# Quarter-array score products for left-over queries, and an earlier time table for the first batch, in a top-k attention and hard-swish kernel

## Chip, cores and metric

The kernel runs on one core of a Trainium2 chip. The metric is device time in microseconds (us); lower is better.

## The reference

Attention over 8 batches of 8 heads with 576 positions and a head dimension of 64, in float32, keeps only the 32 largest scores of each query; a two-layer feed-forward with a hard-swish follows.

```python
scores = scale * np.matmul(q, k.transpose(0, 1, 3, 2))
kth = np.partition(scores, -top_k, axis=-1)[..., -top_k:-top_k + 1]   # top_k = 32
scores = np.where(scores >= kth, scores, -1000000000.0)
attn = np.exp(scores - np.max(scores, axis=-1, keepdims=True))
attn = attn / (np.sum(attn, axis=-1, keepdims=True) + 1e-09)
x = np.matmul(attn, v)        # (B,H,S,D) -> (B*S, H*D) = (4608, 512)
h = x @ w_in                  # 512 -> 2048
g = h * np.clip(h + 3.0, 0.0, 6.0) / 6.0
out = g @ w_out               # 2048 -> 512
```

## The kernel before

**Pairs and duos.** A `Pair` is two heads of one batch: head 0 lies on partitions 0 to 63, head 1 on 64 to 127. Of 576 positions 512 make four tiles of 128 (J = 4), and R = 64 are left over. A `Duo` is two pairs (u = 0 and 1) and one tile of 128 queries, so it has four rows of 576 scores per partition; a left-over duo (`rest`, qt = J) holds the 64 left-over queries of both pairs' heads, head 0 on partitions 0 to 63 and head 1 on 64 to 127, so it has only two rows. A batch has 8 full and 2 left-over duos, 80 in all, numbered m. In batches 0 to 2 the two left-over duos are the batch's last (m = 8 and 9 in the first), in batches 3 to 6 they are spread, in the last they come early.

**The stages of a duo**, by engine: the scores on TensorE (PE) (`scores`; L215 and L217 for left-over duos, L226 and L232 for full ones) and their copy out of PSUM on ScalarE (ACT) (L219 and L220, L233 and L236); the top 32 on VectorE (DVE) in four rounds of MAX8 and MATCH_REPLACE8 (L250, L254); a shift on GpSimd (POOL) (L263, L266); Prelu and Exp with the sum on ACT (L273, L278, L283); the reciprocal on DVE (L287); the weights' product and a split into 16-bit halves on POOL (L297, L306); a DMA transpose on SP's queue (L312); joining the halves on ACT for u = 0 and on POOL for u = 1 (L318); the product with the values on PE (L338) and its copy on ACT (L348).

**The feed-forward** of a block of 128 tokens is 16 pieces: four times 32 products L365, ACT's L373 and L375 and POOL's gate L379 and L380, then 32 products of 128x512 (L385), the scaling on ACT (L395) and the store on SP (L397).

**The weights** arrive in a wide form and are converted in 32 chunks of 128x512 in the first 153 us, one step of each per slot: ACT takes the absolute value (L108) and a second part (L111), POOL clamps (L109), DVE shifts and merges (L117, L118), POOL adds (L123). The chunks' `a` and `y` tiles and the feed-forward's `g` share a pool of 8 buffers.

**Order.** Every engine works its instructions in the order in which the program issues them (`manual_schedule`). The main loop goes over the duos; each has 8 slots, in each of which DVE gets one round of top-k for one u (slots 0 to 3 for u = 0, 4 to 7 for u = 1). A full duo's slot takes some 2.4 us on DVE, a left-over duo's some 1.4 us. What follows a duo's top-k is written into tables by slot, counted from the duo's first: a stage at 9 is issued in slot 1 of the next duo. `early` holds for duos 0 and 1, `usual` for the rest of the first batch, `behind` (as `usual`, with the values at 25) for the middle, `soon` for the last two. In the first four duos all stages but the reciprocals and weights are issued before the slot's conversion step, these two after it. Feed-forward pieces are issued at a rate that follows how many are queued (`due`); what is left at the end follows without top-k beside it.

Of the kernel before, what the change touches and what calls it, by code (L numbers as in the profile page):

```python
# [29 lines left out]
def kernel(  # L30
# [9 lines left out]
    nc = tc.nc  # L40
    P = nc.NUM_PARTITIONS
    B, H, S, D = q.shape
    DM, FF = moe_w_in.shape
    J = S // P
    JP = J * P
    R = S - JP
# [41 lines left out]
    def big():  # L88

        return ps_big.tile([P, 5 * 512], F32, tag="big", name="big")  # L90
# [48 lines left out]
    class Pair:  # L139


        def __init__(self, b, hp):
            self.b, self.hp = b, hp
            self.vm, self.vr, self.kr = vms[hp], vrs[hp], krs[b % 2 * NHP + hp]
# [40 lines left out]
    class Duo:  # L185
# [3 lines left out]

        def __init__(self, pairs, qt):
            self.pairs, self.qt, self.early = pairs, qt, False
            self.rest = qt == J
            self.nt = 1 if self.rest else 2
            self.nb = J + 2 if self.rest else 2 * J + 1
            self.m, self.less = [None] * 2, [None] * 2
            self.e16, self.t16, self.eT = [None] * 2, [None] * 2, [None] * 2

        def scores(self, us=(0, 1)):  # L200

            if us[0] == 0:
                self.sc = scpool.tile([P, 2, 2 * (S + R)], F32, tag="sc", name="sc")
                self.den = mpool.tile([P, 2, 2], F32, tag="den", name="den")
            sc, nu = self.sc[:, us[0] : us[-1] + 1, :], len(us)
            ps = big()
            heads = [slice(0, D), slice(D, P)]
            qs = slice(self.qt * P, min(self.qt * P + P, S))
            banks = ps[:, 0 : 4 * 512].rearrange("p (n s) -> p n s", s=512)
            left = ps[:, 4 * 512 :]  # L210
            if self.rest:
                for i, u in enumerate(us):
                    pr = self.pairs[u]
                    for d in heads:
                        nc.tensor.matmul(banks[d, i, :], pr.qT[d, qs], pr.kT[d, :])  # L215
                    for hh, d in enumerate(heads):
                        nc.tensor.matmul(left[d, i * R : (i + 1) * R], pr.qT[d, qs], pr.kr[d, hh, :])  # L217
                nc.gpsimd.memset(sc[:, :, S : S + R], 0.0)
                nc.scalar.copy(sc[:, :, 0:JP], banks[:, 0:nu, :])  # L219
                nc.scalar.copy(  # L220
                    sc[:, :, JP:S], left[:, 0 : nu * R].rearrange("p (u r) -> p u r", r=R)
                )
                return
            for i, u in enumerate(us):
                pr = self.pairs[u]
                nc.tensor.matmul(  # L226
                    left[:, i * P : (i + 1) * P], pr.qT[:, qs], pr.kr[:].rearrange("p h r -> p (h r)")
                )
            for i, u in enumerate(us):
                pr = self.pairs[u]  # L230
                for hh, d in enumerate(heads):
                    nc.tensor.matmul(banks[:, 2 * i + hh, :], pr.qT[d, qs], pr.kT[d, :])  # L232
            nc.scalar.copy(  # L233
                sc.rearrange("p u (h s) -> p (u h) s", h=2)[:, :, 0:JP], banks[:, 0 : 2 * nu, :]
            )
            nc.scalar.copy(  # L236
                sc[:, :, JP : JP + P], left[:, 0 : nu * P].rearrange("p (u r) -> p u r", r=P)
            )
# [87 lines left out]
        def values(self, dst):  # L326

            w = R if self.rest else P
            pv = ps_w.tile([P, 512], F32, tag="w", name="pv")
            for u in range(2):  # L330
                pr, eT = self.pairs[u], self.eT[u]
                for c in range(J + 1):
                    for hh in range(2):
                        if self.rest:
                            rhs = eT[:, c if c < J else J + hh, hh * R : (hh + 1) * R]
                        else:
                            rhs = eT[:, c if hh == 0 or c == J else J + 1 + c, :]
                        nc.tensor.matmul(  # L338
                            pv[hh * D : (hh + 1) * D, u * w : (u + 1) * w],
                            pr.vm[:, hh, c, :] if c < J else pr.vr[:, hh, :],  # L340
                            rhs,
                            start=(c == 0),
                            stop=(c == J),
                        )
            self.pv = dst, pv[:, 0 : 2 * w].rearrange("p (u q) -> p u q", u=2)
# [70 lines left out]
    per_batch = 2 * J + 2  # L416
    ND = len(duos)
# [4 lines left out]
    left = 0  # L422
# [87 lines left out]
    def pair_at(m, first):  # L510

        b, at = divmod(m, per_batch)
        return pairs[b + 1][at - first] if b + 1 < B and 0 <= at - first < NHP else None
# [18 lines left out]
    usual = dict(  # L532
        shift0=3, exp0=4, inverse0=9, weights0=10, flip0=12, join0=15,
        shift1=7, exp1=8, inverse1=13, weights1=14, flip1=16, join1=19, values=22, place=23,
    )

    behind = dict(usual, values=25, place=26)
    early = dict(
        shift0=3, exp0=3, inverse0=4, weights0=4, flip0=5, join0=8,
        shift1=7, exp1=7, inverse1=8, weights1=8, flip1=9, join1=12, values=12, place=13,  # L540
    )
    soon = dict(
        shift0=3, exp0=3, inverse0=5, weights0=5, flip0=7, join0=10,
        shift1=7, exp1=7, inverse1=9, weights1=9, flip1=11, join1=14, values=16, place=17,
    )
    queued = {}
    for m in range(ND):
        for part, at in (early if m < 2 else soon if m >= ND - 2 else behind if per_batch <= m < ND - 4 else usual).items():
            queued.setdefault(8 * m + at, []).append((m, part))

    def parts(slot, late=None):

        for m, part in sorted(queued.get(slot, []), key=lambda x: x[1][:-1] != "shift"):
            if late is not None and (part[:-1] in ("inverse", "weights")) != late:
                continue
            if part == "values":
                values(m)
            elif part == "place":
                place(m)
            else:  # L560
                getattr(duos[m], part[:-1])(int(part[-1]))

    due = 0.0
    for m in range(ND + 3):
        u = duos[m] if m < ND else None
        for i in range(8):
# [18 lines left out]
            if i == 0:  # L585
                p = pair_at(m, 4)
# [5 lines left out]
            if i == 5:  # L592
                p = pair_at(m, 5)
# [42 lines left out]
```

## Time and profile before

| | us |
|---|---|
| median of 8 runs | 1581.54 (1580.07 to 1583.55) |
| the profiled execution | 1581.16 |
| its span in the profile | 1579.3 |
| DVE busy | 1467.0 (93%) |
| PE busy | 1455.3 (92%) |
| POOL busy | 1143.7 (72%) |
| ACT busy | 1096.0 (69%) |
| largest group: L250 MAX8 `m<-wk`, x864 | 613.6 |
| L385 MATMUL `acc<-w_out,g`, x1152 | 517.7 |
| L365 MATMUL `h<-xT,w_in`, x4096 | 483.1 |
| L215 MATMUL `big<-kq` 64x512, x128 | 32.8 |

How to read it: a float32 product leaves two MATMUL records, and their ends are modelled, so the time of one is better read from start to start. Engines work in order; a line of a timeline gives start, length, engine, source line, operation, tiles, shapes and count, and in brackets the idle time before it and the engine whose work ended that wait. Idle time of an engine counts only where what it delays is waited for in turn.

### The profile page before, as it was taken

The numbers are of one execution on the slowest core, as the hardware profiler recorded it, in microseconds if no ns is written. First come the engines' busy times: TensorE is split into PE (matmuls) and PEld (weight loads), VectorE is DVE, ScalarE is ACT, GpSimd is POOL, SyncE is SP. The second block draws the span as 40 slices with busy tenths as digits, with TensorE's granted clock in tenths as the row PEclk, the third lists the DMA queues.
The fourth block names the chain that finished last, engine by engine and source line by source line (L and its number), as shares of the span: only waits on it lengthen the run. The fifth ranks groups of instructions, "written<-read, shape, count | busy, mean of one in ns | idle before, by whom it ended". The sixth has DMA issues, their size and how long they took to land.

```text
span 1579.3 us, 28787 instructions
## 1 busy us (share of the span) xinstructions
PE 1455.3 (92%) x10272; PEld 1037.2 (66%) x10272; DVE 1467.0 (93%) x3105; ACT 1096.0 (69%) x1865; POOL 1143.7 (72%) x1264
## 2 busy tenths in 40 slices
PE   5355799879999999998999999999999999999899
PEld 3152666567767777776777777776777767677675
DVE  6999999999999999999999999999999999999700
ACT  6675777777776777777776786777766787777621
POOL 4868687777867777767687777777687777767841
PEclk9577899989999999999999999999999999999999
DMA  8652544444444543545244443446344443533400
GB/s 236 160 180 45 113 83 86 89 91 97 76 96 86 98 83 78 103 86 119 55 103 79 99 89 75 93 96 119 51 94 88 98 88 73 104 66 68 83 22 14
DMA packets 450319, 144.49 MB, mean 91 GB/s; under 512 B 433280, under 2 KB 441472, under 8 KB 450176
## 3 DMA queue, kind: packets, MB, share of 16 engines
q1 hardware_dynamic: 450176, 142.65, 43.2%
q8 instruction: 81, 1.33, 0.3%
q14 instruction: 62, 0.51, 0.1%
HBM read 45.09 MB, written 9.44 MB: 35 GB/s over the span
## 4 chain that ended last, share of the span: by engine, by line
DVE 50%; PE 38%; POOL 4%; issue 3%; ACT 2%; SPq 1%; DMA 1%; POOLq 0%; DVEq 0%; ACTq 0%
DVE m L250 26%; DVE wk L254 22%; PE h L365 15%; PE acc L385 14%; PE pv L338 4%; PE big L232 3%; DVE y L118 1%; POOL e L306 1%; PE big L177 1%; DVE a L117 1%; POOL sc L297 1%; POOL eT L318 1%; PE big L215 1%; ACT sc L278 1%; PE big L226 1%
## 5 line engine op out<-in xcount | busy, mean ns | idle before, releaser
L250 DVE MAX8 m<-wk 128x8 f32<-128x576 f32 x864 | 613.6, 747 | 2.2
L385 PE MATMUL acc<-w_out,g 128*128 128x512 f32 x1152 | 517.7, 601 | 17.1 <-POOL g L380 17.1
L365 PE MATMUL h<-xT,w_in 128*128 128x128 f32 x4096 | 483.1, 279 | 17.3 <-ACT xT L348 17.3
L365 PEld LDWEIGHTS h<-xT,w_in 128*128 128x128 f32 x4096 | 472.7, 194 | 39.6 <-issue 18.7
L254 DVE MATCH_REPLACE8 wk<-m,wk 128x576 f32<-128x576 f32 x576 | 424.0, 743 | 0.0
L385 PEld LDWEIGHTS acc<-w_out,g 128*128 128x128 f32 x1152 | 213.7, 191 | 263.8 <-issue 239.4
L297 POOL TENSOR_SCALAR sc<-sc,den 128x576 f32<-128x576 f32 x288 | 213.5, 752 | 219.7 <-DVE den L287 212.6
L306 POOL COPY e<-sc 128x2304 uint16<-128x2304 uint16 (+1 forms) x192 | 320.2, 1678 | 10.1
L278 ACT ACTIVATE sc<-sc,shift 128x576 f32<-128x576 f32 x288 | 220.4, 769 | 35.8 <-POOL shift L266 32.8
L318 ACT COPY eT<-t 128x2304 uint16<-128x2304 uint16 (+1 forms) x82 | 215.9, 2633 | 36.5 <-DMA t<-e 35.6
L273 ACT ACTIVATE sc<-sc,m 128x576 f32<-128x576 f32 x288 | 210.1, 777 | 44.5 <-DVE m L250 44.4
L338 PE MATMUL pv<-eT,vm 128*64 128x128 f32 (+1 forms) x2560 | 163.3, 272 | 55.3 <-ACT eT L318 43.9
L254 DVE MATCH_REPLACE8 wk<-m,sc 128x576 f32<-128x576 f32 x288 | 212.0, 743 | 0.0
L318 POOL COPY eT<-t 128x2304 uint16<-128x2304 uint16 (+1 forms) x78 | 203.8, 2612 | 6.9 <-DMA t<-e 6.6
L250 DVE MAX8 m<-sc 128x8 f32<-128x576 f32 x288 | 203.4, 743 | 1.9 <-ACT sc L236 1.9
L338 PEld LDWEIGHTS pv<-eT,vm 128*64 128x64 f32 x2560 | 134.4, 140 | 106.7 <-ACT eT L318 49.7
L373 ACT ACTIVATE g<-h,three 128x512 f32<-128x512 f32 x144 | 98.5, 684 | 150.4 <-PE h L365 139.7
L380 POOL TENSOR_TENSOR g<-g,hs 128x512 f32<-128x512 f32 x144 | 184.9, 1284 | 12.1 <-POOL g L379 0.2
L379 POOL TENSOR_SCALAR g<-g 128x512 f32<-128x512 f32 x144 | 89.2, 619 | 75.0 <-ACT g L373 65.4
L233 ACT COPY sc<-big 128x2048 f32<-128x2048 f32 (+1 forms) x65 | 119.3, 1836 | 27.3 <-PE big L232 27.2
L232 PE MATMUL big<-kq 64*128 64x512 f32 x512 | 136.1, 652 | 0.0
L395 ACT ACTIVATE o<-acc 128x512 f32<-128x512 f32 x36 | 21.4, 595 | 109.9 <-PE acc L385 109.9
(47 smaller groups left out, 1115.9 us busy)
## 6 DMA issues: line engine op xcount, KB each, us to landing
landed<-in_k_dram SPq DMA_DIRECT2D x64, 128.0 KB, 2.8
landed<-in_q_dram SPq DMA_DIRECT2D x64, 128.0 KB, 2.9
st<-in_moe_w_in_dram SPq DMA_DIRECT2D x16, 512.0 KB, 5.0
vm<-in_v_dram SPq DMA_DIRECT2D x64, 128.0 KB, 2.3
st<-in_moe_w_out_dram SPq DMA_DIRECT2D x16, 512.0 KB, 6.6
out_dram<-o SPq DMA_DIRECT2D x32, 256.0 KB, 2.4
t<-e SPq DMA_TRANSPOSE x160, 4.6
landed<-in_k_dram SPq DMA_DIRECT2D x32, 32.0 KB, 2.6
```

Source lines behind the costliest of these rows:

```text
L232: nc.tensor.matmul(banks[:, 2 * i + hh, :], pr.qT[d, qs], pr.kT[d, :])
L250: nc.vector.max(self.m[u][:, t, 8 * r : 8 * r + 8], self.cur[t])
L254: nc.vector.match_replace(wk, self.m[u][:, t, 8 * r : 8 * r + 8], self.cur[t], LOWEST)
L273: nc.scalar.activation(row, row, AF.Prelu, bias=m[:, t, TOP_K - 1 : TOP_K], scale=-1.0, alpha=FLAT)
L278: nc.scalar.activation(row, row, AF.Exp, bias=self.less[u][:, t : t + 1], scale=-scale / FLAT, accum_out=self.den[:, u, t : t + 1],)
L297: nc.gpsimd.tensor_scalar(row, row, self.den[:, u, t : t + 1], 1.0, ALU.mult, ALU.mult)
L306: nc.gpsimd.tensor_copy(halves[:, :, to : to + c1 - c0], words)
L318: copy(eT[:, 0 : self.nb, :] .rearrange("p c q -> p (c q)") .bitcast(U16) .rearrange("p (x h) -> p h x", h=2), self.t16[u][:, 0 : 2 * self ...
L338: nc.tensor.matmul(pv[hh * D : (hh + 1) * D, u * w : (u + 1) * w], pr.vm[:, hh, c, :] if c < J else pr.vr[:, hh, :], rhs, start=(c == 0), ...
L365: nc.tensor.matmul(h[:, (f - f0) * P : (f - f0 + 1) * P], w_in[:, i, f * P : (f + 1) * P], xT[:, i, :], start=(i == 0), stop=(i == NHP - 1),)
L380: nc.gpsimd.tensor_tensor(g[:], g[:], hs[:], ALU.mult)
L385: nc.tensor.matmul(acc[:], gs[f // nf][:, f % nf * P : (f % nf + 1) * P], w_out[:, f, :], start=(f == 0), stop=(f == NFC - 1),)
```

## The change

Two edits.

**Scores of left-over duos.** Before, pair u wrote its two heads' products to bank u: rows 0 to 63 of the array to columns 0 to 63, and rows 64 to 127 to columns 64 to 127, pair after pair, each followed by its two small products into a fifth bank. Now the second pair's heads change places on the output (`heads[u ^ hh]`): its head 0 goes to columns 64 to 127 and its head 1 to columns 0 to 63. The four 64x512 products use the four quarters of the array and are issued one after another, then the four small ones, into banks 2 and 3. The rows of the second pair are therefore swapped, and `values` reads them back with `(u ^ hh)`.

**The table of the first batch.** Duos 2 to 9 get a table `tight` in place of `usual`. Duos 0 and 1 keep `early`; `behind`, `usual` and `soon` hold for the others as before.

```diff
             if self.rest:
-                for i, u in enumerate(us):
-                    pr = self.pairs[u]
-                    for d in heads:
-                        nc.tensor.matmul(banks[d, i, :], pr.qT[d, qs], pr.kT[d, :])
-                    for hh, d in enumerate(heads):
-                        nc.tensor.matmul(left[d, i * R : (i + 1) * R], pr.qT[d, qs], pr.kr[d, hh, :])
+                quarters = [
+                    (i, hh, d, heads[u ^ hh])
+                    for i, u in enumerate(us)
+                    for hh, d in enumerate(heads)
+                ]
+                for i, hh, d, to in quarters:
+                    pr = self.pairs[us[i]]
+                    nc.tensor.matmul(banks[to, i, :], pr.qT[d, qs], pr.kT[d, :])
+                for i, hh, d, to in quarters:
+                    pr = self.pairs[us[i]]
+                    nc.tensor.matmul(banks[to, 2 + i, 0:R], pr.qT[d, qs], pr.kr[d, hh, :])
                 nc.gpsimd.memset(sc[:, :, S : S + R], 0.0)
                 nc.scalar.copy(sc[:, :, 0:JP], banks[:, 0:nu, :])
-                nc.scalar.copy(
-                    sc[:, :, JP:S], left[:, 0 : nu * R].rearrange("p (u r) -> p u r", r=R)
-                )
+                nc.scalar.copy(sc[:, :, JP:S], banks[:, 2 : 2 + nu, 0:R])
...
-                            rhs = eT[:, c if c < J else J + hh, hh * R : (hh + 1) * R]
+                            rhs = eT[:, c if c < J else J + hh, (u ^ hh) * R :][:, 0:R]
...
+    tight = dict(
+        shift0=3, exp0=3, inverse0=8, weights0=8, flip0=10, join0=13,
+        shift1=7, exp1=7, inverse1=11, weights1=11, flip1=13, join1=16, values=19, place=20,
+    )
     queued = {}
     for m in range(ND):
-        for part, at in (early if m < 2 else soon if m >= ND - 2 else behind if per_batch <= m < ND - 4 else usual).items():
+        if m < per_batch:
+            when = early if m < 2 else tight
+        elif m < ND - 4:
+            when = behind
+        else:
+            when = soon if m >= ND - 2 else usual
+        for part, at in when.items():
             queued.setdefault(8 * m + at, []).append((m, part))
```

For comparison, the table that duos 2 to 9 had:

```python
usual = dict(
    shift0=3, exp0=4, inverse0=9, weights0=10, flip0=12, join0=15,
    shift1=7, exp1=8, inverse1=13, weights1=14, flip1=16, join1=19, values=22, place=23,
)
```

## The prediction

> **What bounds the kernel now.** I read the busy table by 40 us windows first, then VectorE's (DVE's) waits, then the timelines around each wait, then the end. Columns of the windows: stretch, length, busy us and count of PE, weight loads, DVE, ACT, POOL, then granted TensorE clock, DMA share, GB/s.
>
> ```profile
> 120.00:160.00 40.00, 22.45 (x64) 9.41 (x62) 36.69 (x74) 22.91 (x39) 32.56 (x33) 0.79 0.26 51
> ...
> 480.00:520.00 40.00, 40.00 (x277) 27.95 (x277) 40.00 (x87) 28.75 (x48) 29.40 (x32) 1.00 0.44 82
> ...
> 1520.00:1560.00 40.00, 40.00 (x270) 32.35 (x269) 0.00 (x0) 8.88 (x16) 12.16 (x14) 1.00 0.04 14
> ```
>
> In the middle PE and DVE are both full; at the end only PE works. Which of the two is the bound is told by DVE's idle times. These are all of them over 0.3 us between its first and its last top-k; the bracket holds the idle time before the instruction and who ended it.
>
> ```profile
> 137.07 1.48 DVE L117 TENSOR_SCALAR a<-a 128x512 uint32<-128x512 uint32 x1 [3.31 <-POOL a L109]
> ...
> 1181.26 0.17 DVE L287 RECIPROCAL den<-den 128x2 f32<-128x2 f32 x1 [1.02 <-ACT den L283]
> ...
> 1270.65 0.17 DVE L287 RECIPROCAL den<-den 128x2 f32<-128x2 f32 x1 [0.53 <-ACT den L283]
> ...
> 1372.19 0.16 DVE L287 RECIPROCAL den<-den 128x1 f32<-128x1 f32 x1 [1.46 <-ACT den L283]
> 1375.36 1.42 DVE L250 MAX8 m<-sc 128x8 f32<-128x576 f32 x2 [0.69 <-ACT sc L236]
> ```
>
> So from 13.5 us to the last top-k's end at 1492 us DVE is the bound: it loses 3.31 us once in the weight conversion and 3.70 us (1.02+0.53+1.46+0.69) late. The end hangs on it by a string of fixed length. In PE's timeline:
>
> ```profile
> 1496.56 1.25 PE L338 MATMUL pv<-eT,vm 128*64 128x128 f32 x16 [4.41 <-POOL eT L318]
> ```
>
> That POOL copy stands right behind the weights of the last duo on POOL's queue, and those wait for DVE's reciprocal at 1487.9. From 1496.6 on PE works some 80 us without a gap. The time is therefore DVE's arrival at its last duo plus a constant, as long as PE has its older work done (4.41 us in hand). What PE saves is worth only what it takes out of DVE's waits.
>
> **Part 1, four quarter products.** A left-over duo's scores on PE, before:
>
> ```profile
> 204.37 1.07 PE L215 MATMUL big<-kq 64*64 64x512 f32 x4
> 205.28 0.28 PE L217 MATMUL big<-kr,kq 64*64 64x64 f32 x4
> 205.40 1.03 PE L215 MATMUL big<-kq 64*64 64x512 f32 x4
> 206.26 0.28 PE L217 MATMUL big<-kr,kq 64*64 64x64 f32 x4
> 206.47 7.13 PE L385 MATMUL acc<-w_out,g 128*128 128x512 f32 x16
> ```
>
> A float32 product makes two records, so x4 is two products. Two of 64x512 take 0.91 us (204.37 to 205.28) and the next thing starts at 206.47: 2.10 us in all. One full-array 128x512 product takes 0.86 us (L385: 8 records in 3.44 us in the chain), so the two quarters (first rows to first columns, second to second) already run together. That two column halves run together on different moving data is shown by L338: 40 records, 20 products, in 2.33 us, 0.12 us each, where a 128-column L365 product takes 0.22 us (64 in 14.29 us). Four at once is shown nowhere. Bounds: all four overlap, about 0.95 us for the large and 0.12 for the small ones, 1.07 us, 1.03 us saved; or the second pair doesn't overlap the first, 2.10 us, nothing saved. Worse than nothing is excluded: the new order begins with the same two diagonal quarters side by side. Both halves of the evidence being in the trace, I take 1.03 us, x16 duos = 16.5 us of PE.
>
> The Trainium skill, "TensorEngine Tiling (Array Packing)", section "Gotcha 1: PSUM Pressure", says that different row tiles can't access the same PSUM bank at the same time. The old pair does put both row tiles into one bank (on different partitions) and takes 0.91 us, not 1.7, so the row speaks against the rule. By the rule the two products of a bank would not overlap, and the new order, whose neighbours share a bank, would save nothing: the sum would be that of the third rival.
>
> Of the 16.5 us the time sees only DVE's 3.70. PE has not idled between 1094 us and 1485; left-over scores stand at 1158, 1247, 1337 and 1355, so PE is 1, 2 and about 4 us early at the waits. At 1181 the reciprocal waits for exps behind ACT's output scaling, which waited 4.94 us for PE: 1.0 earlier covers 1.02. At 1270 the chain is PE h, ACT g, eT copy, exps: 2 us covers 0.53. At 1372 the value loads on SP's queue (1358.3 to 1362.8, released by PE's pv) hold up the transpose that feeds ACT's eT copy: 2 to 3 us earlier covers 1.46 and then 0.69. I take 3.4 of 3.7; bounds 0 and 3.7. The copies behind the scores keep their sizes (1.01 and 0.28 us) and are hidden on ACT.
>
> **Part 2, the tighter table, duos 2 to 9.** By the order listing it moves work only in the first 310 us: beyond the 675th matmul of 5282, the 241st POOL and the 367th DVE instruction the orders are the same but for the quarters; on SP one store and one transpose change places. PE's feed-forward starts earlier, but PE idles anyway until 327 us (9.31 us there), so that is worth nothing, and the tail holds the same work as before. What counts is DVE up to 310 us. Its one wait comes like this, on POOL and ACT:
>
> ```profile
> 125.66 2.15 POOL L297 TENSOR_SCALAR sc<-sc,den 128x576 f32<-128x576 f32 x2
> 127.87 2.10 POOL L306 COPY e<-sc 128x2304 uint16<-128x2304 uint16 x1
> 130.06 1.40 POOL L379 TENSOR_SCALAR g<-g 128x512 f32<-128x512 f32 x1
> 131.54 1.26 POOL L380 TENSOR_TENSOR g<-g,hs 128x512 f32<-128x512 f32 x1
> ...
> 134.54 0.69 ACT L373 ACTIVATE g<-h,three 128x512 f32<-128x512 f32 x1 [9.12 <-POOL w_out L123]
> ```
>
> POOL's weights and gate delay its add (L123, 133.2 to 134.5), which frees a buffer for ACT's g; behind g stands ACT's abs of a weight chunk (135.59), then POOL's clamp (136.42), then DVE's shift (137.07). After the change the same queue, walked with these durations: clamp to 116.1, weights (now two slots earlier) to 117.6, split to 119.7, gate to 121.7, add to 123.0; abs 0.7, clamp 0.6, add 1.3 to 125.6; ACT's score copies hold the next abs to 126.9; clamp, gate, shift, add to 131.3; ACT's g and hs to 132.6, 2.9 us earlier than before. But the exps of duo 3 now stand ahead of the abs (1.44, 1.9 and 0.2 us): 136.1, abs 136.7, clamp 137.3. DVE's wait stays, about 0.3 longer. Then the second half's weights of duo 2, three slots earlier, come between that clamp and the next add: 2.15 + 2.10 to 141.6, add 142.9, clamp 143.5; the next conversion on DVE, at 141.91 before, starts at 143.5. Cost 1.6 us. Bounds: -3.3 (the wait goes) and +4.3 (a whole weights and split, 2.15 + 2.10, added to it).
>
> The reciprocals move too: the second half's from five slots behind its exps to four, 9.7 us behind the top-k, or 5.6 where those slots are a left-over duo's. DVE then waits for ACT if den is later, and all later top-k queue behind it. Before, den came 2.6 to 5.8 us after the top-k's end in duos 4 to 7 (5.4 for duo 7: top-k ends at 221.8, den at 227.2) and 6.7 for the second half of duo 8. Against 9.7 that is covered; against 5.6, twice, it costs 0 to 1.1 each. I take 0.5, bounds 0 and 2.2.
>
> **Sum**, on the profiled execution (span 1579.3, 1581.16 with 1.9 outside it): 1579.3 - 3.4 + 1.6 + 0.5 = 1578.0, so 1579.9. The median of the 8 runs lies 0.4 above that execution: 1580.2.
>
> **Rivals.** Within 0.2% means 1578.4 to 1584.7, about what a measurement of this kernel can tell from no change.
> 1. Forecast, late waits go, the early queue gives some back: 1580.2; 0.32.
> 2. The early queue is no worse or loses its wait: -3.4 with 0 early gives 1578.1, -3.7 and -3.3 give 1574.5. For it: g is free 2.9 us earlier, and if the exps' 3.5 us ran beside something else the wait would be gone. Against: ACT is in order. 0.30.
> 3. The quarters run two at a time, the late waits stay: 1581.5 + 2.1 = 1583.6; 0.12, still within 0.2%.
> 4. Slower: the earlier reciprocals make DVE wait for ACT in the first batch. For it: the second half of duo 3 had its den 10.5 us after its top-k (144.18 to 154.66), more than the 9.7 now allowed. Price: 0.8 there, 2.2 at the left-over duos, up to 4.3 in the conversion: 7.3, less 3.4, is 1585.4; without the late gain 1588.8. It decides once the early loss passes 3.2 us plus what the late waits give. 0.26.
>
> So faster 0.30, same 0.44, slower 0.26. The range 1573.8 to 1586.0 leaves out the far part of case 4 and the edge of 2; case 1's own is 1578.4 to 1582.5.
>
> **What would show it.** Right: L215 at x8 in about 1.0 us; DVE's waits at 1181 to 1375 gone; DVE's wait for POOL's clamp still about 3.5 us; duo 4's first top-k (144.18) at 145 to 147; PE's last gap before pv at 4 us or more. Wrong: L215 x8 still near 2 us; new waits of DVE for den before 300 us over 1 us; a tail after that gap other than 80 us.

## The result, and the profile after

The changed kernel takes 1585.7 us (median of 11 runs, 1584.0 to 1586.5), the kernel before 1580.7 us (31 runs on the same chip): ratio 1.0030, 95% interval 1.0022 to 1.0037. It is slower by 0.3%. The profiled execution has a span of 1584.0 us (1579.3 before) and a granted TensorE clock of 0.956 (0.963 before).

**The quarters work.** In PE's timeline of the changed kernel a left-over duo's scores now look like this:

```profile
211.71 1.09 PE L222 MATMUL big<-kq 64*64 64x512 f32 x8
212.62 0.29 PE L225 MATMUL big<-kr,kq 64*64 64x64 f32 x8
212.84 3.70 PE L391 MATMUL acc<-w_out,g 128*128 128x512 f32 x8
```

Eight records, four products, from 211.71 to 212.62: 0.91 us, what two took before. The whole block takes 1.13 us to the next instruction, against 2.10 us.

**DVE lost time early and won it late.** All idle times of DVE over 0.3 us between 100 us and the last top-k, in DVE's timeline of the changed kernel (the bracket holds the idle time before the instruction):

```profile
125.28 1.48 DVE L117 TENSOR_SCALAR a<-a 128x512 uint32<-128x512 uint32 x1 [2.46 <-POOL a L109]
...
138.27 0.43 DVE L117 TENSOR_SCALAR a<-a 128x512 uint32<-128x512 uint32 x1 [4.17 <-POOL a L109]
...
144.68 0.43 DVE L117 TENSOR_SCALAR a<-a 128x512 uint32<-128x512 uint32 x1 [2.61 <-POOL a L109]
...
245.99 0.16 DVE L293 RECIPROCAL den<-den 128x1 f32<-128x1 f32 x1 [4.02 <-ACT den L289]
```

The four late waits at 1181 to 1375 us are gone (-3.70). In the conversion there are three waits, 9.24 us, in place of one of 3.31 (+5.93), and a new one of 4.02 us at the second half of duo 8. Sum: +6.25. The two conversion instructions themselves got shorter, 52.2 us busy in all against 55.2 (L117 and L118 in the groups by line), so about 3 us came back. Most of that had come back before the first wait, so the two nearly cancel: DVE is ready for the 29th of the 32 L117 at 122.82 us and, after 2.46 us, begins it at 125.28; before, it began it at 125.78 without a wait. The time is lost at the second and third waits: duo 4's first top-k begins at 147.37 us, before at 144.18. DVE ends its last top-k at 1495.7 us, before at 1492.2: +3.6. The rest of the span follows in 88.3 us (before 87.2).

Two stretches by windows show the place; the columns are those of the prediction's first fence:

```profile
120.00:160.00 40.00, 23.43 (x95) 11.73 (x94) 30.77 (x62) 21.27 (x33) 31.70 (x32) 0.80 0.23 45
...
1520.00:1560.00 40.00, 40.00 (x250) 30.26 (x247) 0.00 (x0) 8.03 (x15) 9.40 (x10) 1.00 0.04 14
```

Between 120 and 160 us DVE works 30.77 us instead of 36.69; the tail is full of PE work, as before.

**How the conversion waits come about.** POOL's timeline ahead of the first of them, changed kernel:

```profile
115.99 2.04 POOL L303 TENSOR_SCALAR sc<-sc,den 128x576 f32<-128x576 f32 x2
118.09 2.10 POOL L312 COPY e<-sc 128x2304 uint16<-128x2304 uint16 x1
120.28 0.67 POOL L385 TENSOR_SCALAR g<-g 128x512 f32<-128x512 f32 x1
121.03 1.59 POOL L386 TENSOR_TENSOR g<-g,hs 128x512 f32<-128x512 f32 x1
122.58 1.26 POOL L123 TENSOR_TENSOR w_out<-a,y 128x512 int32<-128x512 int32 x1
124.63 0.62 POOL L109 TENSOR_SCALAR a<-a 128x512 f32<-128x512 f32 x1 [0.79 <-ACT a L108]
```

Weights, split and gate stand ahead of the add (L123), which frees the buffer that ACT's abs needs; then come abs, clamp, and only then DVE. The second wait has another maker. ACT's timeline ahead of it:

```profile
132.66 0.69 ACT L379 ACTIVATE g<-h,three 128x512 f32<-128x512 f32 x1 [4.41 <-POOL w_out L123]
...
133.72 1.45 ACT L279 ACTIVATE sc<-sc,m 128x576 f32<-128x576 f32 x2
...
136.82 0.65 ACT L108 ACTIVATE a<-st 128x512 f32<-128x512 f32 x1
```

Between 133.72 and 136.82 ACT does the exps of duo 3, which the tight table puts one slot earlier, ahead of the abs: 3.1 us. The third is again POOL's: weights at 138.33, split at 140.61, add at 142.68, clamp at 144.03.

**How the wait at duo 8 comes about.** ACT's timeline, changed kernel:

```profile
239.86 2.79 ACT L324 COPY eT<-t 128x2304 uint16<-128x2304 uint16 x1 [1.27 <-DMA t<-e]
242.51 1.01 ACT L179 COPY kq<-big 128x1024 f32<-128x1024 f32 x1
...
243.98 0.78 ACT L279 ACTIVATE sc<-sc,m 128x576 f32<-128x576 f32 x1
...
245.75 0.20 ACT L289 ACTIVATE den<-den 128x1 f32<-128x1 f32 x1
```

The top-k of that half ended at 236.3 us. Its exps start at 243.98, because ACT's queue holds the join of duo 7 ahead of them, which waits for its DMA transpose, and behind the join the copies L179 to L183 (1.5 us). The same join stood ahead of the same exps before, as ACT's timeline of the kernel before shows, but there the exps followed it at once:

```profile
235.04 2.80 ACT L318 COPY eT<-t 128x2304 uint16<-128x2304 uint16 x1 [0.54 <-DMA t<-e]
237.71 0.77 ACT L273 ACTIVATE sc<-sc,m 128x576 f32<-128x576 f32 x1
```

There that top-k ended at 233.0 us. The join starts 3.6 us after the top-k in place of 2.0, and from its start to the exps it is 4.1 us in place of 2.7: together the 3.0 us by which den is later (9.7 us after the top-k, 6.7 before). The transpose is late because duo 7's weights began on POOL only at 231.59, 5.1 us after their reciprocal (226.50): a gate and another join stood ahead of them. POOL's timeline, changed kernel:

```profile
226.93 0.62 POOL L385 TENSOR_SCALAR g<-g 128x512 f32<-128x512 f32 x1 [1.27 <-ACT g L379]
...
228.84 2.80 POOL L324 COPY eT<-t 128x2304 uint16<-128x2304 uint16 x1
231.59 1.50 POOL L303 TENSOR_SCALAR sc<-sc,den 128x576 f32<-128x576 f32 x2
```

### The profile page after: what moved, and what is told of

It reads as the page before. It is cut to its first block, busy times and chain, and to the rows that moved or that the text cites. A ratio compares the mean times of both kernels' runs of the same rounds, so it can differ in the third digit from the quotient of the medians.

```text
span 1584.0 us, 28784 instructions
## 1 busy us (share of the span) xinstructions
PE 1445.6 (91%) x10272; PEld 1035.9 (65%) x10272; DVE 1464.2 (92%) x3105; ACT 1098.1 (69%) x1865; POOL 1144.9 (72%) x1264
## 4 chain that ended last, share of the span: by engine, by line
DVE 77%; PE 8%; POOL 6%; issue 4%; ACT 2%; SPq 1%; DMA 1%; POOLq 0%; ACTq 0%
DVE m L256 41%; DVE wk L260 36%; PE h L371 4%; PE acc L391 4%; POOL e L312 1%; POOL a L109 1%; POOL sc L303 1%; ACT sc L284 1%; PE pv L344 1%; POOL eT L324 1%; POOL w_in L123 1%; DVE den L293 1%; DMA st<-in_moe_w_in_dram 1%; POOL w_out L123 1%; SPq L151 0%
## 5 line engine op out<-in xcount | busy, mean ns | idle before, releaser
L371 PE MATMUL h<-xT,w_in 128*128 128x128 f32 x4096 | 487.5, 280 | 20.3 <-ACT xT L354 20.3
L371 PEld LDWEIGHTS h<-xT,w_in 128*128 128x128 f32 x4096 | 477.0, 196 | 42.0 <-ACT xT L354 21.6
L381 ACT COPY hs<-h 128x512 f32<-128x512 f32 x144 | 83.5, 580 | 0.0
```

The costliest lines, as they stand in the source:

```text
L371: nc.tensor.matmul(h[:, (f - f0) * P : (f - f0 + 1) * P], w_in[:, i, f * P : (f + 1) * P], xT[:, i, :], start=(i == 0), stop=(i == NHP - 1),)
```

## Experiments

Theory after the result: the two edits are independent; the quarters take DVE's late waits away, the table gives back more than that in the conversion and at duo 8. For each run: DVE's waits between 100 us and the last top-k, that top-k's end, and what follows it to the end of the span, all from its profiled execution; the ratio is to the kernel before on the same chip (its medians there are 1580.6 to 1581.5 us).

| kernel | median us | ratio (95%) | DVE waits | last top-k ends | rest |
|---|---|---|---|---|---|
| before | 1580.7 | | 7.0 | 1492.2 | 87.2 |
| changed | 1585.7 | 1.0030 (1.0022, 1.0037) | 13.3 | 1495.7 | 88.3 |
| quarters alone | 1577.8 | 0.9979 (0.9970, 0.9988) | 3.3 | 1488.7 | 87.9 |
| table alone | 1589.8 | 1.0054 (1.0042, 1.0067) | 18.0 | 1500.8 | 87.8 |
| quarters, table for 2 and 3 | 1581.1 | 1.0001 (0.9992, 1.0009) | 9.2 | 1491.4 | 87.2 |
| quarters, table for 4 to 9 | 1579.5 | 0.9991 (0.9982, 1.0000) | 5.1 | 1490.2 | 88.0 |
| changed, duo 7's join later | 1582.6 | 1.0006 (0.9998, 1.0015) | 10.8 | 1494.2 | 87.9 |
| table for 2 and 3, exps at old slots | 1579.8 | 0.9991 (0.9983, 1.0000) | 6.9 | 1490.5 | 88.0 |
| table for 2 and 3, weights at old slots | 1581.3 | 1.0000 (0.9991, 1.0009) | 8.6 | 1492.1 | 87.3 |
| quarters issued twice | 1580.9 | 0.9997 (0.9988, 1.0006) | 6.3 | 1491.5 | 87.2 |
| quarters, other order (one execution) | 1577.5 | | 3.3 | 1487.9 | 87.8 |
| quarters, PE's gaps filled | 1572.7 | 0.9946 (0.9934, 0.9959) | 3.3 | 1488.7 | 82.2 |
| old scores, PE's gaps filled | 1575.5 | 0.9967 (0.9955, 0.9979) | 6.9 | 1492.3 | 82.2 |
| the former, with quarters and duo 2's weights later | 1569.3 | 0.9925 (0.9912, 0.9937) | 0.3 | 1485.2 | 82.2 |

The last two columns carry the case: the rest is 87.2 to 88.3 us wherever the tail's work is the same, so the time is DVE's arrival plus a constant, as predicted. Top-k end less waits is 1485.1 us before and 1485.4 with the quarters alone; over all kernels it is 1484.7 to 1485.4 where duos 2 and 3 have the old table and 1482.2 to 1483.7 where they have the tight one or a part of it. That goes with the conversion instructions (L117 and L118), which take 54.9 to 55.3 us in the former and 52.3 to 53.6 in the latter.

### The two edits apart

Quarters alone, and the table alone (with the scores of before):

```diff
-            when = early if m < 2 else tight
+            when = early if m < 2 else usual
```

> The quarter products with the old table. Theory A (the quarters took DVE's late waits away): DVE's waits at 1181, 1270, 1372 and 1375 us go, 3.7 us in all, the early wait of 3.3 us stays; 1580.7 - 3.7 = 1577.0 us, between 1576.5 and 1578. Theory B (the late waits went in the changed kernel because the table made DVE some 5 us later at them, so that PE was no longer behind): the waits stay here and the time is that of before, 1580.7 us within 1.

> The tight table with the old score products. Early waits of DVE as in the changed kernel: 2.5, 4.2 and 2.6 us in the conversion and 4.0 us at the second half of duo 8. Theory A, the table has no part in the late waits: they stay, and the time is the changed kernel's 1585.7 + 3.7 = 1589.4 us. Theory B, the delay itself removes them: 1585.7 us, the same as the changed kernel.

Measured: 1577.8 and 1589.8 us, within 1 us of theory A in both; theory B falls. With the quarters alone no wait of DVE is left between 138 us and the last top-k. With the table alone the late waits of 1.05, 0.52, 1.46 and 0.69 us are there, shifted by 9 us, so it is not DVE's delay that removes them. Its waits at duos 7 and 8, from DVE's timeline of that kernel:

```profile
231.71 0.17 DVE L287 RECIPROCAL den<-den 128x2 f32<-128x2 f32 x1 [0.93 <-ACT den L283]
...
247.23 0.17 DVE L287 RECIPROCAL den<-den 128x1 f32<-128x1 f32 x1 [4.13 <-ACT den L283]
```

### The table in two halves

```diff
-            when = early if m < 2 else tight
+            when = early if m < 2 else tight if m < 4 else usual      # the first
+            when = early if m < 2 else usual if m < 4 else tight      # the second
```

> Quarters, the tight table for duos 2 and 3 alone, the old one for 4 to 9. If the conversion waits come from duos 2 and 3, whose exps and weights stand in ACT's and POOL's queues ahead of the conversion's: all three conversion waits (2.5, 4.2, 2.6 us) stay, the 4.0 us at duo 8 goes, and the time is 1585.7 - 4.0 = 1581.7 us. Rival, that the loss of the changed kernel is one delay handed on, so that taking the later duos back changes nothing: 1585.7 us.

> Quarters, the old table for duos 2 and 3, the tight one for 4 to 9. If the theory of places holds: the conversion has its one old wait of 3.3 us, the reciprocal of duo 8 waits 4.0 us, the late waits are gone; 1580.7 - 3.7 + 4.0 = 1581.0 us. Rival, that the wait at duo 8 is there only because the early delay shifted ACT's queue against DVE's: it is gone and the time is 1577.0 us.

Measured: 1581.1 and 1579.5 us. The first has the three conversion waits (2.46, 4.17, 2.60) and nothing at duo 8, as the theory of places has it. The second has the old 3.31 and a wait at duo 8 that is less than half of what was expected:

```profile
240.51 0.16 DVE L293 RECIPROCAL den<-den 128x1 f32<-128x1 f32 x1 [1.82 <-ACT den L289]
```

So both halves cost something by themselves (over quarters alone: 3.3 and 1.7 us), and 2.9 us of the changed kernel's 7.9 are there only with both; 2.2 of these are in the wait at duo 8 (4.02 against 1.82). The profiles say where: with the table for 4 to 9 alone duo 7's weights start on POOL 1.9 us after their reciprocal (223.23, 225.09), in the changed kernel 5.1 us after it, as shown above. The join right ahead of them is there in both (222.33, 228.84), the gate ahead of that join only in the changed kernel.

### The join at duo 8

```diff
             when = early if m < 2 else tight
+            if m == 7:
+                when = dict(tight, join0=16)
```

> The changed kernel, with the first half of duo 7 joined three slots later (behind the exps of duo 8's second half in ACT's queue, not ahead of them). Theory: the 4.02 us that DVE waits at duo 8's reciprocal come from ACT's eT copy, which waits for its transpose by DMA while those exps stand behind it; with the copy behind them the wait goes, and the time is 1585.7 - 4.0 = 1581.7 us. Rival: a reciprocal four left-over slots behind its exps is too early in itself, whatever stands in between; at least 2 us of the wait stay, 1583.7 us or more.

Measured 1582.6 us, 3.1 less than the changed kernel (the theory said 4.0, the rival at most 2.0). Of the 4.02 us, 1.36 stay, and 0.15 appear at the next duo's scores:

```profile
244.13 0.16 DVE L293 RECIPROCAL den<-den 128x1 f32<-128x1 f32 x1 [1.36 <-ACT den L289]
```

The exps no longer wait for the transpose. What now holds them, by ACT's timeline of this run, is POOL's shift, which stands behind a split and a gate:

```profile
243.00 0.77 ACT L284 ACTIVATE sc<-sc,shift 128x576 f32<-128x576 f32 x1 [1.33 <-POOL shift L272]
```

The join was the larger part, not the whole.

### Exps or weights

Both on the kernel with quarters and the tight table for duos 2 and 3 alone:

```diff
-            when = early if m < 2 else tight if m < 4 else usual
+            when = early if m < 2 else dict(tight, exp0=4, exp1=8) if m < 4 else usual   # exps at old slots
+            when = early if m < 2 else dict(usual, exp0=3, exp1=7) if m < 4 else usual   # the rest at old slots
```

> Quarters, and for duos 2 and 3 the tight table with the exps one slot later, as in the old one; the old table for 4 to 9. Beside the run with the tight table for duos 2 and 3 (1581.1 us; conversion waits 2.46, 4.17, 2.60 us). Theory: only the 4.17 us come from the exps, which stand ahead of the conversion's abs on ACT for 3.1 us; they fall to about 1.1, the others stay, 1578.0 us. Rival: ACT's abs waits for a buffer that POOL's add frees anyway, so that the exps run in a hole: the waits add up to the same, 1581 us.

> Quarters, and for duos 2 and 3 the old table with the exps one slot earlier, as in the tight one: reciprocals, weights and all behind them at the old slots. Theory: the 2.46 and 2.60 us come from POOL's weights and split (2.0 + 2.1 us), which stand ahead of its add in the tight table; they go, and one wait of about 3.3 (that of the old table) to 4.2 us stays: 1577.8 to 1578.7 us. Rival: the exps ahead of the abs add their 3.1 us to the old table's wait of 3.3: 1581 us.

Measured 1579.8 and 1581.3 us. With the exps back the wait of 4.17 us fell to 1.11, as expected, but the first rose from 2.46 to 3.14, and 1.3 us of the 3.1 expected were gained. The waits fell by 2.4 us in all, but the conversion instructions took 0.9 us longer (53.5 against 52.6). With the weights back the theory fails and the rival's time holds. One wait is left, and it is longer than either foresaw:

```profile
139.19 1.48 DVE L117 TENSOR_SCALAR a<-a 128x512 uint32<-128x512 uint32 x1 [8.58 <-POOL a L109]
```

Over quarters alone (1577.8) the early exps cost 3.5 us by themselves, the early weights (with reciprocals and all behind them) 2.0, both 3.3. It is one loop, from POOL's add over the freed buffer to ACT's abs, POOL's clamp and DVE: either edit alone is enough to lengthen it, and the costs don't add.

### Is it PE's time that removes the late waits?

```diff
-                for i, hh, d, to in quarters:
+                for i, hh, d, to in quarters + quarters:
```

> Quarters with the old table, but the four large products of each left-over duo are issued twice (the second set writes the same values again): some 0.9 us of PE more for each of 16 duos, about what the quarters had saved. Theory: DVE's late waits at 1181 to 1375 us come back, 3.7 us, and the time is that of before, 1580.8 us (1580 to 1582). Rival: the gain of the quarters came from elsewhere (copies, order), and PE has room: 1577.8 us.

Measured 1580.9 us. In PE's timeline the large products now take 1.77 us (204.34 to 206.11):

```profile
204.34 1.95 PE L222 MATMUL big<-kq 64*64 64x512 f32 x16
206.11 0.29 PE L225 MATMUL big<-kr,kq 64*64 64x64 f32 x8
```

Late waits of 0.30, 1.28 and 0.69 us are back (that at 1181 us is not, a new one of 0.75 us at 420 us is), and the time with them. PE's 0.9 us per left-over duo are what the quarters give. Which of the late waits appear differs between executions of the same order: the kernel with old scores and filled gaps (below) is the kernel before up to its last duo, and its profile has none at 1181 and 1270 us, 1.42 and 0.69 us at 1372 and 1375, and this one:

```profile
421.29 0.17 DVE L287 RECIPROCAL den<-den 128x1 f32<-128x1 f32 x1 [1.48 <-ACT den L283]
```

PE reaches one and the same instruction at 369.64 us there and at 367.90 in the profile before, while DVE is only 0.3 us later. The late waits add up to much the same in both, 3.59 and 3.70 us.

### Does the overlap hang on the order?

```diff
-                    for i, u in enumerate(us)
                     for hh, d in enumerate(heads)
+                    for i, u in enumerate(us)
```

> Quarters with the old table, but issued in another order: both pairs' first heads (the same rows, different columns, different PSUM banks), then both second heads. If the overlap does not depend on which quarters are neighbours: 8 records in about 0.9 us as before and the same time, 1577.8 us within 0.2%. If neighbours on the same rows get in each other's way, or if sharing a bank does: not 0.9 us but up to 1.8 us, and some of the late waits come back.

It does not: 8 records in 0.91 us again (204.07 to 204.98), the same wait of 3.29 us, 1577.5 us in one run.

### PE's gaps ahead of the tail

Three feed-forward pieces are issued earlier, where PE idles for the joins of duos 77 and 78:

```diff
             due -= int(due)
+            if m == ND - 1 and i in (5, 7):
+                piece(i // 2 - 1)
```

> Quarters with the old table throughout, and three pieces of the feed-forward (some 1.8 us of PE each) issued earlier, in slots 5 and 7 of the last duo, where PE idles 2.39 and 4.45 us for the joined weights of duos 77 and 78. Theory (the end is PE's unbroken work behind those gaps, so PE time saved by the quarters is worth something only where it lets work be moved up): 1577.8 - 5.4 = 1572.4 us. Rival: the gates that these pieces bring stand ahead of the join on POOL and push the gaps back by 1.9 us each: 1574.3 to 1576.2 us.

> The kernel before, old scores and old table, with the three feed-forward pieces in slots 5 and 7 of the last duo. It tells whether the 5.1 us that filling gave were made by the quarters or were there already. Before, PE idles 0.26 us ahead of duo 77's values and 4.41 us ahead of duo 78's, 4.67 in all, against 2.39 + 4.45 = 6.84 with the quarters. Theory 1, the gap is filled in either kernel: 1581.0 - 4.4 = 1576.6 us. Theory 2, without the quarters PE is behind by what they save, so pieces put ahead of the values only delay what stands behind: 1581.0 us or up to 2 more.

Measured 1572.7 and 1575.5 us: 5.1 us less than the same kernel without the filling, in both. The gain is therefore not the quarters'; the gap was there before. DVE's last top-k does not move; the rest falls to 82.2 us in both, from 87.9 and 87.2. PE's timeline with the quarters:

```profile
1482.70 1.09 PE L344 MATMUL pv<-eT,vm 128*64 128x128 f32 x16 [2.18 <-ACT hs L381]
...
1491.10 1.98 PE L391 MATMUL acc<-w_out,g 128*128 128x512 f32 x4 [0.44 <-ACT hs L381]
```

Then, on top of filling and quarters, the wait of the old table. Duo 2's first weights move behind the conversion's last steps:

```diff
             when = early if m < 2 else usual
+            if m == 2:
+                when = dict(usual, weights0=13, flip0=14, join0=17)
```

> Quarters, the old table, the gaps of PE at the end filled (1572.7 us), and the first half of duo 2 gets its weights three slots later (with flip and join), behind the last conversion steps that DVE waits for. Theory: the 3.31 us that DVE waits in the conversion come from POOL's weights and split (some 4 us) ahead of its add; without them the wait goes, and as DVE's arrival is what sets the end the time is 1572.7 - 3.3 = 1569.4 us. Rival 1: the exps of duo 3 ahead of the abs keep 1 to 3 us of it, 1570.5 to 1572.5. Rival 2: DVE's time no longer sets the end once PE's gaps are filled: 1572.7 us.

Measured 1569.3 us, against 1569.4 expected. DVE's only wait left between 100 us and its last top-k:

```profile
138.47 0.43 DVE L117 TENSOR_SCALAR a<-a 128x512 uint32<-128x512 uint32 x1 [0.31 <-POOL a L109]
```

This version beats both kernels: 0.75% under before, 1.0% under the changed one (1569.3 to 1585.7). It moves the weights of one half of duo 2 later, where the change moved them earlier.

## Why the prediction was wrong, step by step

**What bounds the kernel: right.** Over all versions with the old tail the span is DVE's arrival plus 87.2 to 88.3 us.

**Part 1: right.** Four quarters take 0.91 us, and a left-over duo saves 0.97 us of PE where 1.03 were expected; 3.4 us were taken, 3.4 us came (last top-k 1492.2 to 1488.7; the medians give 3.0). The rule of the Trainium skill that spoke against it ("TensorEngine Tiling (Array Packing)", "Gotcha 1: PSUM Pressure") does not hold for these products: two row tiles write to one bank, on different partitions, and overlap in both orders tried. The Trainium skill, "PSUM — Partial Sum Buffer", "PSUM bank collisions raise a hardware error", quotes the same rule, but the clash of two row tiles that it reports as measured is at the same 32 partitions of one bank, which these products avoid; that agrees with the 0.91 us.

**Part 2: the places were right, the size too small.** "Cost 1.6 us" turned out as 3.2 (duo 4's first top-k from 144.18 to 147.37 us, just beyond the 145 to 147 that were given). The walk foresaw the exps ahead of the abs (a wait of 3.6, measured 4.17) and the second half's weights ahead of an add (1.6, measured 2.61). Its durations on POOL were too short, 1.5 us for the weights at 116 us (2.04) and 2.0 for the gate behind them (2.34), so its clamps end at 137.3 and 143.5 us where they ended at 138.23 and 144.64. It has no wait at 125 us, though its own clamp there ends at 124.3: DVE was there at 122.82, some 3 us earlier than before, because its conversion instructions had got shorter, which no step had. That gain and that wait nearly cancel.

**The reciprocals: the step that failed.** "I take 0.5, bounds 0 and 2.2" was 4.02 us, beyond its bound. The step set a fixed lateness of den (6.7 us after the top-k in the old profile) against a shorter allowance (5.6), which makes 1.1 us. But den did not stay where it was: it came 9.7 us after the top-k (236.3 to 245.95). The 3.0 us more are ACT's: the join ahead of those exps starts 1.6 us later after the top-k, as its weights came later on POOL, and copies that stood ahead of the join before (231.35) now stand between it and the exps, 1.5 us. Putting the join behind the exps took 2.66 of the 4.02 us away. The lateness of one stage was read from the old queue and used in the new one.

**The sum.** In its own terms, -3.4 + 1.6 + 0.5 became -3.7 + 3.2 + 4.0, and the tail, put at nothing, 1.1: together 4.6 of the 4.7 us by which the span grew. Rival 4's 1585.4 us is almost the result, and its sign is right, but not its parts: the 0.8 us at duo 3 did not occur, the left-over duos cost 4.0 instead of 2.2, the conversion 3.2 instead of 4.3. That the number is so near is luck. It should have had the larger chance; its two prices were upper bounds of steps that I had put at 1.6 and 0.5.

**The tail: held, with a small loss.** PE's gap ahead of duo 78's values is 4.45 us (4.41 before), and behind it the string is 83.9 us instead of 82.7; the granted clock behind the gap is lower (0.50 from 1500 to 1505 us; before, 0.87 from 1490 to 1500 and 0.92 from 1500 to 1505). The three groups of products behind the gap (the values x16 and x4, then L371 x32) take 7.59 us there and took 6.51 before, which makes 1.1 us of that difference (last section).

Open: why PE comes later to the same instruction in one execution than in another, and with it why the late waits fall at 420 us in one and at 1181 in another; and how the early half of the table brings the gate ahead of the join and of duo 7's weights. The profile shows that it is there, no run took it away.

## What to carry to other kernels

When a time table is tightened, walk every engine's queue anew: the lateness of a value belongs to the queue that stood ahead of it, and what stands ahead of it (here a join that waits for a DMA, and copies) may come later than it did. Time saved on an engine that is not the bound is worth the bound's waits for it and no more: some 15.5 us of PE (16 times 0.97) gave 3. Once the bound and a constant tail are known, look at what fills the tail; three pieces issued earlier gave 5.1 us, more than the quarters' 3.

## What the hardware showed

**PE is slow after its gap.** In PE's timeline of the changed kernel the values behind the 4.45 us gap take 1.97 us, where the same x16 takes 1.09 elsewhere (1.75 and 0.93 from start to start):

```profile
1500.13 1.97 PE L344 MATMUL pv<-eT,vm 128*64 128x128 f32 x16 [4.45 <-POOL eT L324]
```

The granted clock is 0.50 between 1500 and 1505 us, and 0.92 in the next 5 us. With the gaps filled (2.18 and 0.44 us are left) it stays at 1.00 from 1470 to 1530 us. That is why the filling shortened the span by 5.7 us, though PE's idle time fell by only 3.6 (6.84 us to 2.18, 0.44 and a later 0.65). With the quarters alone the three groups behind the gap take 7.14 us (1493.13 to 1500.27; clock 0.60 and 0.71 in the two stretches of 5 us from 1490), and the same three 10.77 us earlier take 5.01 (1482.36 to 1487.37): the difference of 2.1 us is the rest. The length of the gap alone does not tell the loss: before, behind 4.41 us, the three took 6.51. The Trainium skill, "TensorE: Matmul & The Clock Gate", "What's actually happening", gives half the clock after an idle window of some 3.4 us; the 0.50 behind 4.45 us agrees.

**DVE and POOL hold each other up.** DVE's L117 takes 0.41 us with nothing on POOL (107.22 before) and 1.48 us at 125.28 in the changed kernel, beside POOL's add that starts at 125.21 and takes 1.27 us. At 138.27 it goes first and takes 0.43 us, and POOL's weights, which start at 138.33, take 2.22 us instead of 1.47. These 0.75 us are more than what was left of L117 (0.37), so L118, on DVE until 139.29, must have a part in them; no run takes the two apart. The 32 L117, 13 us at 0.41 each, cost 21.6 us in the changed kernel and 25.0 before; in both, each that takes over 0.6 us begins while a POOL instruction runs. The Trainium skill, "SBUF — State Buffer", "Who interferes with whom", calls it an exclusive lock that the first to start keeps; the first case agrees with that, the second if L118 keeps it too.
